# A fifth buffer of attention weights, sums copied before the next rounding, loads moved inside chunks, and a memset moved to VectorE, in a fused attention and mixture-of-experts kernel

## The chip, the cores and the metric

The kernel runs on one core of a Trainium2 chip. The metric is the device time of one execution in microseconds (us). TensorE (PE in the profile, PEld for its weight loads), VectorE (DVE), ScalarE (ACT), GpSimd (POOL) and SyncE (SP) run side by side and wait for each other by semaphores. SP only issues transfers here (DMA); POOL issues those that go by index.

## The reference

```python
B, S, D, d_qk = 8, 2496, 256, 64            # u, v: (B, S, D); z: (B, S, d_qk)
scores = (1.0 / S) * (z @ z.transpose(0, 2, 1))
attn = np.maximum(scores, 0.0) ** 2
x = (u * (attn @ v)).reshape(B * S, D)
out = x.copy()
...                                          # only tokens with x @ w_skip > 0:
e_idx = argmax(xc @ w_gate)                  # one of 8 experts for each token
gate_w = softmax(xc @ w_gate)[e_idx]
out = xc + gate_w * (np.maximum(xc @ w1[e], 0.0) @ w2[e])   # w1: 256x1024, w2: 1024x256
```

All of it is float32. The kernel keeps this precision by splitting each operand of a product into a high part (a cast to the rounded type fp32r) and a low part (the operand less its high part), and by adding three products: high by high, high by low, low by high.

## The kernel before, in words

**Attention.** A batch has 2496 tokens. Its queries are cut into five chunks, four of 512 and one of 448 (`chunks`, 40 in all, called chunk 0 to 4 of batch 0 to 7 below). Its keys are cut into ten pairs of 256 (`NP` = 10), and one chunk with one pair is a step: 400 steps. Steps are numbered from 0 in a chunk, and through the program from 0 to 399; step 80 is step 0 of chunk 3 of batch 1. `ORDER` says in which order a chunk takes its pairs.

The weights of a step, `relu(z z^T / S)^2`, are symmetric. So eight blocks of a batch (`PAIRS`) are computed once, turned by DVE (`keep`, tile `rt`), written to DRAM (`kept`) by SP, and read back (`recall`) when the mirrored block is due. The other steps are computed: `scores` on PE into PSUM (`ps`), relu and square on ACT into `r` (lines 290 and 291). For either kind the rounding follows: `high` casts `r` to `ah` (line 313, on ACT or DVE as `on_act` says) and `low` subtracts on DVE to get `al` (line 317). `attend` (line 341) multiplies `ah` and `al` with `vh` and `vl` into the sums `acc`. Its index d picks one half of the features, so a step calls it twice, and each half has two accumulators (t = 0 and 1), for the two halves of TensorE's rows.

`weights` for a step is called two steps ahead (`LA` = 2), `recall` five steps ahead. At a chunk's end `finish` evacuates: for each d, `part(d, 1)` copies one accumulator to `xrow` by ACT (line 369) and `part(d, 0)` adds the other by DVE (line 371). Only then may the next chunk's `attend` of that d start, because all accumulators of PSUM are in use. Then `mul` multiplies by `ut` (u, loaded one chunk ahead), `rows0` and `rows1` turn the result, and `store` writes it.

**Queues.** Each engine runs its own instructions in the order in which the program was written (`manual_schedule`); `todo` and `at` set work to a half-step number, which is run at the end of that step. So whatever waits holds up all that was written behind it on that engine. This goes for SP too, which issues a transfer only when its target buffer is free.

**Loads.** z and v of the next batch are loaded and split in the background (`load_z`, `load_v`): SP starts the transfer, and seven half-steps later ACT casts (lines 108 and 119) and DVE subtracts (lines 109 and 120). `load_w` does the same for the weights of the experts.

**Routing and experts.** After every second chunk the tokens are routed: `gates` multiplies by the gate's weights on PE, `logits` turns the result to `lg` (lines 431 and 435; where a chunk has 448 tokens, line 434 fills the rest with zeros), `route` finds the expert (`mx` to `hot`), `counts` and `place` find its place in the expert's list (`pre`, and a product with a triangle on PE, line 476), and `put_in` writes token numbers to the lists by POOL. After the attention comes the experts' part, in units of 256 tokens: `h_part` 0 to 3 (line 598), then `y_part` (line 617), with other work put between these parts by `fills`, whose number says after which part. The first unit's tokens were listed early, and the last chunk's routing is done in the fills of this unit.

The loop over steps, as far as it is touched:

```python
if k < NP - 1:                      # all steps but the last of a chunk
    high, low = stage(s + LA)
    high()
    low()
    for d in range(2 if k < NP - 2 else 1):
        attend(b, n, p, d, acc[d], *aa[s], k == 0, False)
```

Of the kernel before, what the change touches and what calls it, by code (L numbers as in the profile page):

```python
# [8 lines left out]
F32 = mybir.dt.float32  # L9
# [8 lines left out]
P = 128  # L18
QC = 512
# [28 lines left out]
def attn_moe(ctx, tc, zT, uT, v, wg, w1, w2, cst, pad, out):  # L48
# [113 lines left out]

    def load_u(ci):
        b, q0, n = chunks[ci]
        uts[ci] = xp.tile([P, 2, QC], F32, name="ut", tag="ut", bufs=4)
        nc.sync.dma_start(uts[ci][:, :, :n], uT[b, :, :, q0 : q0 + n])

    warm = cpool.tile([P, 1], F32, name="warm")
# [83 lines left out]
        return ps  # L252

    def r_tile():
        return ap.tile([P, 2, QC], F32, name="r", tag="r", bufs=4)

    turned_r, puts, step = {}, [], [0]

# [135 lines left out]
    def routing(cis, rows64=True):  # L394
# [27 lines left out]
        def logits():  # L422

            ps = psg.pop()
            lgf = lg.rearrange("p t c -> p (t c)")
            same = all(n % P == 0 for n in ns)
            for g, n in [(0, ns[0])] if same else enumerate(ns):
                full = 32 * (n // P)
                w = P * len(ns) if same else P
                o = g * P  # L430
                nc.vector.transpose(lgf[:full, o : o + w], ps[:full, o : o + w])
                if n % P:
                    k = o + n % P
                    nc.gpsimd.memset(lgf[full : full + 32, k : o + P], 0.0)
                    nc.vector.transpose(lgf[full : full + 32, o:k], ps[full : full + 32, o:k])

        def route():
# [231 lines left out]
    def at(s, f):  # L669

        todo.setdefault(s // 2, []).append(f)
# [3 lines left out]
    def stage(s):  # L675
        if s < len(steps):
            aa[s], high, low = weights(*steps[s], old.pop(s, None))
            return high, low
        return lambda: None, lambda: None
# [16 lines left out]
    def later(s, k, load, *args):  # L696
        def start():
            f = load(*args)
            at(s + k, f)
        at(s, start)  # L700

    for ci, (b, q0, n) in enumerate(chunks):
        s0 = ci * NB
        if ci + 1 < NC:
            at(s0 + 12, lambda ci=ci: load_u(ci + 1))
        if ci == 0:
            first = [(4 * j - 8, j % 2, 3, load_z, j) for j in range(2, NZ)]
            first += [(2 * g - 4, 1, 4, load_v, g) for g in range(2, NB // 2)]
            for s1, _, k, load, j in sorted(first, key=lambda x: x[:2]):
                eng = nc.vector  # L710
                if s1 - k < 0:
                    at(s1, load(0, j, eng))
                else:
                    later(s1 - k, k, load, 0, j, eng)
            at(14, lay_pads)
        if q0 == 0 and b + 1 < B:

            end = s0 + NB * -(-S // QC)
            for j in range(NZ):
                s1 = (s0 + 24, s0 + 44, end - 18, end - 14, end - 10)[j]  # L720
                later(s1, 7, load_z, b + 1, j, nc.vector)
            for g in range(NB // 2):
                s1 = s0 + 21 + 8 * g if g < 7 else (end - 17, end - 14, end - 12)[g - 7]
                later(s1, 7, load_v, b + 1, g, nc.vector)

    s_end = NC * NB
    s_w = s_end - 3 * NB

    def start_w():
        for k, f in enumerate(load_w(0, nc.vector)):  # L730
            at(s_w + 8 + 5 * k, f)

    at(s_w, start_w)

# [20 lines left out]
    for s, (ci, p) in enumerate(steps):  # L755
        b, q0, n = chunks[ci]
        k = s % NP
        step[0] = s
        ahead(s + LA + 3)
        if k == 0:  # L760
            accs[ci] = [[ps_acc.tile([P, QC], F32, name="acc", tag="acc") for _ in range(2)] for _ in range(2)]
        acc = accs[ci]
        if k < NP - 1:
            high, low = stage(s + LA)
            high()
            low()
            for d in range(2 if k < NP - 2 else 1):
                attend(b, n, p, d, acc[d], *aa[s], k == 0, False)
            if k < NP - 2:
                aa.pop(s)  # L770
        else:


            part, mul, rows0, rows1, store = finish(ci)
            attend(b, n, p, 0, acc[0], *aa[s], False, True)
            part(0, 1, acc[0])
            part(0, 0, acc[0])
            high, low = stage(s + LA)
            attend(b, n, steps[s - 1][1], 1, acc[1], *aa.pop(s - 1), False, False)
            if s + LA in known:  # L780

                high()
                low()
                high = low = lambda: None
            attend(b, n, p, 1, acc[1], *aa.pop(s), False, True)
            part(1, 1, acc[1])
            high()
            part(1, 0, acc[1])
            low()
            mul()  # L790
            accs.pop(ci)

            new.append(ci)
            if ci < NC - 1:
                after = [(rows0, 2), (rows1, 3), (store, 4), (store, 5)]
                if ci % 2 == 0:
                    gates, logits, route, counts, gate, place, put_in = routing(new)
                    after = [(gates, 2), (logits, 2), (rows0, 2), (rows1, 3), (route, 4), (counts, 4),
                             (store, 4), (gate, 5), (store, 5), (place, 6)]
                    for t in range(0, 4 * len(new), 2):  # L800
                        f = lambda put_in=put_in, t=t: put_in(t, t + 2)
                        if s + 6 + t < len(steps):
                            after.append((f, 6 + t))
                        else:
                            left.append(f)
                    new = []
                for f, k in after:
                    todo.setdefault(s + k, []).append(f)
            else:
                gates, logits, route, counts, gate, place, put_in = routing(new, False)  # L810
        for f in todo.pop(s, []):
            f()
        put_some()
# [57 lines left out]
    for e in range(E):  # L871
# [3 lines left out]
        for i in range(NFIX):  # L875
# [11 lines left out]
            elif i == 0:  # L887
                add(fills, (0, lambda: turn_pe(pair(0, 1), turned(0, 1))))
                add(fills, (0, gates), (0, rows0), (0, rows1), (0, store), (0, store), (1, logits), (1, route),
                    (2, counts), (2, gate), (3, end_routes), (5, end_lists))  # L890
                add(fills, *zip((0, 2), left))
            elif i == 1:
                add(fills, (1, end_counts), (3, lambda: turn_pe(pair(0, 2), turned(0, 2))), (4, rows(0, 3)), (6, rows(0, 4)))
                add(fills, *zip((1, 3, 5), wq[:3]))
            else:
                add(fills, (1, rows(1, 0)), (3, rows(0, 5)), (4, lambda: turn_pe(pair(0, 3), turned(0, 3))),
                    (5, rows(1, 1)), (6, lambda: load_ids(idts[2], 2, 2 * NSTAT)))
                add(fills, *zip((1, 2, 3, 5, 6), wq[3:]))
# [99 lines left out]
```

## Time and profile before

| what | value |
|---|---|
| time, median of 3 runs | 1835.14 us (1831.97 to 1837.5) |
| profiled execution, time | 1834.64 us |
| its span, first to last instruction | 1832.8 us |
| granted TensorE clock, mean | 0.996 |
| PE busy | 1787.2 us, 98% of the span |
| DVE, ACT, POOL busy | 1182.8, 1159.5, 440.8 us |
| attention, to the last chunk's end | about 0 to 1323 us |
| experts | the rest |

The span is what the profile shows; some 2 us of the execution lie around it. A row of the timeline has the start and the length in us, then the engine, the line of the kernel, the operation, what it writes and reads, and in brackets the idle time of the engine before it and what ended that. A row of waits has the waiting engine with its tile and line, what it waited for, the sum in us, how often, and the longest. Numbers of buffers are left out of names.

### The profile page before, as it was taken

How to read it: one execution, taken by the hardware profiler on the slowest of the kernel's cores; microseconds unless marked ns; L12 is line 12 of the kernel's file. 1: busy time of each engine (PE TensorE's matmuls, PEld its weight loads, DVE VectorE, ACT ScalarE, POOL GpSimd, SP SyncE). 2: the span in 40 equal slices, each digit the busy share in tenths (PEclk: the TensorE clock that was granted, in tenths of full speed). 3: DMA queues.
4: the chain of work that ended last, by engine and by line, in shares of the span. 5: the costliest groups of instructions: out<-in, count | busy, mean ns of one | idle time of the engine just before them, and what ended most of it. 6: DMA issues, size and time to landing. Idle time of an engine off the chain costs nothing. (4 is left out here: it accounts for less than half of the span.)

```text
span 1832.8 us, 40463 instructions
## 1 busy us (share of the span) xinstructions
PE 1787.2 (98%) x15844; PEld 1575.9 (86%) x15844; DVE 1182.8 (65%) x2105; ACT 1159.5 (63%) x1499; POOL 440.8 (24%) x429
## 2 busy tenths in 40 slices
PE   8999999999999999999999999999989999999997
PEld 7888878877887798788879878877889999999997
DVE  6777776876777687678678777867643343334432
ACT  8877876877777687678777876877523233333321
POOL 0102201210220120121012022112254556635621
PEclk9999999999999999999999999999989999999999
DMA  5575687487657847784784787578542233313210
GB/s 185 128 179 138 168 207 190 122 207 187 170 136 196 207 116 193 202 198 119 186 215 108 183 208 187 133 182 197 147 103 76 80 96 106 89 53 94 84 37 26
DMA packets 403766, 267.46 MB, mean 146 GB/s; under 512 B 205859, under 2 KB 334117, under 8 KB 403440
## 3 DMA queue, kind: packets, MB, share of 16 engines
q1 hardware_dynamic: 389440, 240.47, 51.9%
q0 software_dynamic: 13712, 22.99, 4.4%
q8 instruction: 141, 2.31, 0.5%
q14 instruction: 185, 1.52, 0.3%
q10 hardware_dynamic: 288, 0.17, 0.0%
HBM read 145.80 MB, written 118.39 MB: 144 GB/s over the span
## 5 line engine op out<-in xcount | busy, mean ns | idle before, releaser
L341 PE MATMUL acc<-ah,vh 64*128 64x512 f32 (+1 forms) x3120 | 729.5, 387 | 17.5 <-DVE xrow L371 11.4
L341 PE MATMUL acc<-ah,vl 64*128 64x512 f32 (+1 forms) x3120 | 712.7, 385 | 0.0
L317 DVE TENSOR_TENSOR al<-r,ah 128x1024 fp32r<-128x1024 f32 (+3 forms) x464 | 480.0, 1048 | 251.1 <-ACT ah L313 238.8
L341 PE MATMUL acc<-al,vh 64*128 64x512 f32 (+1 forms) x3120 | 562.0, 385 | 3.6 <-DVE al L317 3.2
L341 PEld LDWEIGHTS acc<-ah,vh 64*128 64x128 f32 x3120 | 423.8, 185 | 87.4 <-DVE xrow L371 25.8
L341 PEld LDWEIGHTS acc<-ah,vl 64*128 64x128 f32 x3120 | 424.0, 185 | 45.9 <-DVE vl L120 0.2
L500 POOL DMA_INDIRECT lst<-pair,dest x160 | 192.4, 1203 | 1093.4 <-DVE dest L498 996.1
L290 ACT ACTIVATE r<-ps 128x1024 f32<-128x1024 f32 (+1 forms) x278 | 280.3, 1008 | 225.2 <-PE ps L251 185.3
L341 PEld LDWEIGHTS acc<-al,vh 64*128 64x128 f32 x3120 | 361.3, 185 | 58.6 <-DVE al L317 11.9
L313 ACT CAST ah<-r 128x1024 fp32r<-128x1024 f32 (+3 forms) x381 | 329.1, 891 | 37.8 <-DMA r<-kept 13.2
L291 ACT ACTIVATE r<-r 128x1024 f32<-128x1024 f32 (+1 forms) x278 | 289.9, 1043 | 8.8
L603 ACT ACTIVATE hh<-psh 128x512 fp32r<-128x512 f32 (+1 forms) x172 | 98.7, 584 | 293.2 <-PE psh L598 256.7
L617 PE MATMUL y<-w2t,hh 128*128 128x256 f32 x1328 | 246.5, 287 | 0.0
L598 PE MATMUL psh<-xt,w1h 128*128 128x256 f32 (+1 forms) x1280 | 231.8, 284 | 2.1 <-issue 1.8
L617 PEld LDWEIGHTS y<-w2t,hh 128*128 128x128 f32 x1328 | 208.7, 193 | 1.3 <-issue 1.3
L598 PEld LDWEIGHTS psh<-xt,w1h 128*128 128x128 f32 x1280 | 196.9, 189 | 3.1 <-issue 3.1
L604 DVE SCALAR_TENSOR_TENSOR hl<-psh,hh 128x512 fp32r<-128x512 f32 (+1 forms) x172 | 113.0, 671 | 131.6 <-ACT hh L603 126.0
L617 PE MATMUL y<-w2t,hl 128*128 128x256 f32 x664 | 189.0, 285 | 1.2 <-DVE hl L604 1.2
L598 PE MATMUL psh<-xt,w1l 128*128 128x256 f32 (+1 forms) x640 | 181.1, 283 | 0.0
L268 DVE STREAM_TRANSPOSE rt<-r 128x512 f32<-128x512 f32 x244 | 158.4, 687 | 1.2 <-DMA kept<-rt 1.1
L251 PE MATMUL ps<-zh 64*128 64x512 f32 (+1 forms) x556 | 137.8, 399 | 4.6 <-ACT zh L108 4.6
L251 PE MATMUL ps<-zl,zh 64*128 64x512 f32 (+1 forms) x556 | 135.8, 391 | 0.0
(170 smaller groups left out, 1661.1 us busy)
## 6 DMA issues: line engine op xcount, KB each, us to landing
kept<-rt SPq DMA_DIRECT2D x244, 256.0 KB, 4.9
r<-kept SPq DMA_DIRECT2D x488, 128.0 KB, 4.0
raw<-in_v SPq DMA_DIRECT2D x80, 256.0 KB, 3.8
ut<-in_uT SPq DMA_DIRECT2D x32, 512.0 KB, 5.1
xr<-xrow SPq DMA_DIRECT2D x128, 128.0 KB, 3.1
out<-xrow SPq DMA_DIRECT2D x128, 128.0 KB, 3.2
raw<-in_w SPq DMA_DIRECT2D x64, 256.0 KB, 3.3
zf<-in_zT SPq DMA_DIRECT2D x40, 256.0 KB, 3.8
```

What stands on the lines that cost most here:

```text
L251: nc.tensor.matmul(to, k[h, o : o + P], queries(q, h, n), start=(m == 0), stop=(m == 2))
L268: nc.vector.transpose(t[:, :, 32 * k : 32 * k + 32], r[:, x, :].rearrange("p (m i) -> p m i", i=32))
L290: nc.scalar.activation(r[:, :, :n], ps[:, :, :n], AF.Relu, scale=isc)
L291: nc.scalar.activation(r[:, :, :n], r[:, :, :n], AF.Square)
L313: (nc.scalar.copy if on_act(ci, p) else nc.vector.tensor_copy)(h_, r_)
L317: nc.vector.tensor_sub(l_, r_, f32(h_))
L341: nc.tensor.matmul(acc[t][:, :n], w[h, x, dd], a[h, x, :n], start=(first and t not in halves[:m]), stop=(last and t not in halves[m + 1 :]),)
L500: put = nc.gpsimd.indirect_dma_start(out=lst, out_offset=bass.IndirectOffsetOnAxis(ap=dest[:, t : t + 1], axis=0), in_=pair[:, t, :], in_o ...
L598: nc.tensor.matmul(ps[:, j * W : (j + 1) * W], wt[:, a, o : o + P], x[:, d, :W], start=(m == 0), stop=(m == 5),)
L603: nc.scalar.activation(hh[:, : G * W], ps[:, : G * W], AF.Relu)
L604: nc.vector.scalar_tensor_tensor(hl[:, : G * W], ps[:, : G * W], 0.0, f32(hh[:, : G * W]), op0=ALU.max, op1=ALU.subtract)
L617: nc.tensor.matmul(ys[t], h[:, tt], w2t[f][:, k, :], start=(f == 0 and m == 0 and t % 2 == 0), stop=(f == NF - 1 and m == 2), skip_group_c ...
```

## The change

1. `r` gets five buffers instead of four, `ut` three instead of four; both have 4 KB per partition.
2. At a chunk's last but one step, the rounding (`high`, `low`) of the next chunk's first step is no longer written where it is staged, unless that step is recalled. It is written in the chunk's last step: ahead of `part(0, ...)` where DVE casts, and behind it where ACT casts. That is the case in chunks 2 and 3 of batches 1 to 7, 14 times.
3. The conversions of z and v of the next batch get a table of chunk and step, with none in steps 8, 9, 0 and 1. Before, v was converted in steps 4 and 8 of chunk 1, 2 and 6 of chunk 2, 0, 4 and 8 of chunk 3, and 5 to 7 of chunk 4. The weights of expert 0 likewise.
4. The zeros of `lg` are written by DVE, not POOL.
5. In the first unit of the experts, `place` with the first list writes comes after `y_part` 0 instead of `h_part` 3, and `end_lists` one place later too.

```diff
-        uts[ci] = xp.tile([P, 2, QC], F32, name="ut", tag="ut", bufs=4)
+        uts[ci] = xp.tile([P, 2, QC], F32, name="ut", tag="ut", bufs=3)
...
-        return ap.tile([P, 2, QC], F32, name="r", tag="r", bufs=4)
+        return ap.tile([P, 2, QC], F32, name="r", tag="r", bufs=5)
...
-                    nc.gpsimd.memset(lgf[full : full + 32, k : o + P], 0.0)
+                    nc.vector.memset(lgf[full : full + 32, k : o + P], 0.0)
...
-            end = s0 + NB * -(-S // QC)
-            for j in range(NZ):
-                s1 = (s0 + 24, s0 + 44, end - 18, end - 14, end - 10)[j]
-                later(s1, 7, load_z, b + 1, j, nc.vector)
-            for g in range(NB // 2):
-                s1 = s0 + 21 + 8 * g if g < 7 else (end - 17, end - 14, end - 12)[g - 7]
-                later(s1, 7, load_v, b + 1, g, nc.vector)
+            jobs = [(load_v, 0, 1, 3), (load_z, 0, 1, 6), (load_v, 1, 2, 3), (load_z, 1, 2, 5), (load_v, 2, 2, 7)]
+            jobs += [(load_v, 3, 3, 3), (load_v, 4, 3, 4), (load_v, 5, 3, 6), (load_v, 6, 3, 7)]
+            jobs += [(load_v, 7, 4, 2), (load_z, 2, 4, 3), (load_v, 8, 4, 4), (load_z, 3, 4, 5)]
+            jobs += [(load_v, 9, 4, 6), (load_z, 4, 4, 7)]
+            for load, j, c, k in jobs:
+                later(s0 + c * NB + 2 * k - 7, 7, load, b + 1, j, nc.vector)
...
-        for k, f in enumerate(load_w(0, nc.vector)):
-            at(s_w + 8 + 5 * k, f)
+        for k, f in zip((4, 6, 12, 14, 16, 22, 24, 26), load_w(0, nc.vector)):
+            at(s_w + 2 * k, f)
...
             high, low = stage(s + LA)
-            high()
-            low()
+            if k < NP - 2 or s + LA in known:
+                high()
+                low()
+                high = low = lambda: None
...
+            rest = high, low
         else:
...
             attend(b, n, p, 0, acc[0], *aa[s], False, True)
+
+            high, low = rest
+            if s + 1 < len(steps) and not on_act(*steps[s + 1]):
+                high()
+                low()
+                high = low = lambda: None
             part(0, 1, acc[0])
             part(0, 0, acc[0])
+            high()
+            low()
             high, low = stage(s + LA)
...
-                    (2, counts), (2, gate), (3, end_routes), (5, end_lists))
+                    (2, counts), (2, gate), (4, end_routes), (6, end_lists))
```

ACT at the end of chunk 2 of batch 1, before: `r_3811` is step 79 (the last of the chunk), `r_3861` step 80, `r_3746` the recalled step 81; `vh` is a piece of v for the next batch.

```order
L119 CAST vh_3572<-raw_3570 128x512
L290 ACTIVATE r_3811<-ps_3804 128x1024
L291 ACTIVATE r_3811<-r_3811 128x1024
L313 CAST ah_3814<-r_3811 128x1024
L290 ACTIVATE r_3861<-ps_3854 128x1024
L291 ACTIVATE r_3861<-r_3861 128x1024
L313 CAST ah_3864<-r_3861 128x1024
L369 COPY xrow_3881<-acc_3442 128x512
L313 CAST ah_3905<-r_3746 128x1024
L369 COPY xrow_3881<-acc_3444 128x512
```

The same place in the changed kernel, where `r_3799` is step 79, `r_3851` step 80 and `r_3740` step 81:

```order
L290 ACTIVATE r_3799<-ps_3792 128x1024
L291 ACTIVATE r_3799<-r_3799 128x1024
L313 CAST ah_3802<-r_3799 128x1024
L119 CAST vh_3607<-raw_3605 128x512
L290 ACTIVATE r_3851<-ps_3844 128x1024
L291 ACTIVATE r_3851<-r_3851 128x1024
L369 COPY xrow_3867<-acc_3436 128x512
L313 CAST ah_3882<-r_3851 128x1024
L313 CAST ah_3895<-r_3740 128x1024
L369 COPY xrow_3867<-acc_3438 128x512
```

The first copy of a sum has moved ahead of the cast of step 80, the second still follows the cast of step 81. Of the buffers, which no row here shows: before, step 80's `r` had the place in memory that step 79's had; now it has that of step 78. Likewise step 3 of chunk 4 had the place of step 2, and now has that of step 1.

DVE at the same place, before:

```order
L317 TENSOR_TENSOR al_3762<-r_3758,ah_3761 128x1024
L268 STREAM_TRANSPOSE rt_3690<-r_3758 128x16x32 x2
L120 TENSOR_TENSOR vl_3573<-raw_3570,vh_3572 128x512
L317 TENSOR_TENSOR al_3815<-r_3811,ah_3814 128x1024
L498 TENSOR_SCALAR dest_3438<-df_3719 128x2
L317 TENSOR_TENSOR al_3865<-r_3861,ah_3864 128x1024
L371 TENSOR_TENSOR xrow_3881<-acc_3441,xrow_3881 128x512
L317 TENSOR_TENSOR al_3906<-r_3746,ah_3905 128x1024
L371 TENSOR_TENSOR xrow_3881<-acc_3443,xrow_3881 128x512
L374 TENSOR_TENSOR ut_3308<-xrow_3881,ut_3308 128x1024
```

And in the changed kernel:

```order
L317 TENSOR_TENSOR al_3756<-r_3752,ah_3755 128x1024
L268 STREAM_TRANSPOSE rt_3684<-r_3752 128x16x32 x2
L317 TENSOR_TENSOR al_3803<-r_3799,ah_3802 128x1024
L498 TENSOR_SCALAR dest_3428<-df_3713 128x2
L120 TENSOR_TENSOR vl_3608<-raw_3605,vh_3607 128x512
L371 TENSOR_TENSOR xrow_3867<-acc_3435,xrow_3867 128x512
L317 TENSOR_TENSOR al_3883<-r_3851,ah_3882 128x1024
L317 TENSOR_TENSOR al_3896<-r_3740,ah_3895 128x1024
L371 TENSOR_TENSOR xrow_3867<-acc_3437,xrow_3867 128x512
L374 TENSOR_TENSOR ut_3302<-xrow_3867,ut_3302 128x1024
```

The first add has moved ahead of the `al` of step 80, and `vl` behind the `al` of step 79; the second add still stands behind the `al` of step 81.

PE in the first unit of the experts, before (`psm` is `place`, `y` the unit's output):

```order
L598 MATMUL psh_18806<-xt0_18289,w1l_17854 128x256
L476 LDWEIGHTS tri_127
L476 MATMUL psm_18821<-hot_18672,tri_127 128x32
L476 LDWEIGHTS ones_129
L476 MATMUL psm_18821<-pre_18673,ones_129 128x32
L617 MATMUL y_18702<-w2t_17984,hh_18703 128x256 x2
```

And in the changed kernel:

```order
L617 MATMUL y_18702<-w2t_18043,hh_18703 128x256 x2
L617 MATMUL y_18702<-w2t_18043,hl_18704 128x256
L476 LDWEIGHTS tri_127
L476 MATMUL psm_18833<-hot_18672,tri_127 128x32
L476 LDWEIGHTS ones_129
L476 MATMUL psm_18833<-pre_18673,ones_129 128x32
L617 MATMUL y_18702<-w2t_18340,hh_18703 128x256 x2
```

The twelve matmuls of `y_part` 0 now stand ahead of the two that read `hot` and `pre`.

## The prediction

> **What bounds the kernel now.** I read the page first, then who waited for whom, then the rows around the longest waits of TensorE.
>
> ```profile
> PE 1787.2 (98%) x15844; PEld 1575.9 (86%) x15844; DVE 1182.8 (65%) x2105; ACT 1159.5 (63%) x1499; POOL 440.8 (24%) x429
> ```
> ```profile
> ACT r L290 <- DVE al L317: 20.5, 10, 2.4
> ...
> PE acc L341 <- DVE xrow L371: 11.4, 15, 1.0
> ...
> PE psm L476 <- DVE hot L451: 6.4, 1, 6.4
> ...
> DVE mx L442 <- POOL lg L434: 5.9, 1, 5.9
> ...
> PE acc L341 <- ACT xrow L369: 3.3, 7, 0.5
> PE acc L341 <- DVE al L317: 3.2, 12, 0.3
> ...
> PE psm L476 <- DVE pre L457: 1.2, 1, 1.2
> ...
> PE psm L409 <- ACT r L290: 1.0, 1, 1.0
> ```
>
> TensorE (PE) is busy 98% of the span, so only its waits can give time back, and the change removes no TensorE work. Its waits are few and lie in four places: at chunks' ends it waits for the sums to be copied out of `acc` (11.4 + 3.3), at the entrance to the experts it waits once for `hot` and `pre` (6.4 + 1.2), and now and then for `al`, or for a `ps` buffer. The wait for `hot` is VectorE's (DVE's) wait for the memset on GpSimd (POOL), 5.9. The 20.5 us that ScalarE (ACT) waits for `al` is a wait for a buffer of `r`.
>
> I count a loss from start to start of matmuls, since the idle column begins only at a modelled end: below, 277.88 follows 276.50 by 1.38, and 0.88 of it is called idle.
>
> **Chunks' ends (2 to 3 and 1 to 2 of batches 1 to 7).** First ACT, then DVE, then PE, chunk 2 to 3 of batch 1:
>
> ```profile
> 269.57 1.05 ACT L313 CAST ah<-r 128x1024 fp32r<-128x1024 f32 x1
> 272.77 1.02 ACT L290 ACTIVATE r<-ps 128x1024 f32<-128x1024 f32 x1 [2.14 <-DVE dest L498]
> ...
> 274.92 1.05 ACT L313 CAST ah<-r 128x1024 fp32r<-128x1024 f32 x1
> 275.87 0.58 ACT L369 COPY xrow<-acc 128x512 f32<-128x512 f32 x1
> 276.35 1.05 ACT L313 CAST ah<-r 128x1024 fp32r<-128x1024 f32 x1
> ```
> ```profile
> 271.46 1.22 DVE L317 TENSOR_TENSOR al<-r,ah 128x1024 fp32r<-128x1024 f32 x1
> ...
> 277.14 0.68 DVE L371 TENSOR_TENSOR xrow<-acc,xrow 128x512 f32<-128x512 f32 x1
> 277.74 1.21 DVE L317 TENSOR_TENSOR al<-r,ah 128x1024 fp32r<-128x1024 f32 x1
> 278.87 0.68 DVE L371 TENSOR_TENSOR xrow<-acc,xrow 128x512 f32<-128x512 f32 x1
> ```
> ```profile
> 272.73 0.73 PE L341 MATMUL acc<-al,vh 64*128 64x512 f32 x4
> ...
> 276.50 0.50 PE L341 MATMUL acc<-ah,vh 64*128 64x512 f32 x1 [0.52 <-ACT xrow L369]
> 277.88 0.50 PE L341 MATMUL acc<-ah,vh 64*128 64x512 f32 x1 [0.88 <-DVE xrow L371]
> ...
> 278.22 0.63 PE L341 MATMUL acc<-ah,vh 64*128 64x512 f32 x2
> 278.46 0.63 PE L341 MATMUL acc<-ah,vl 64*128 64x512 f32 x2
> ...
> 279.61 0.72 PE L341 MATMUL acc<-ah,vl 64*128 64x512 f32 x2
> ```
>
> ACT's relu of step 80 starts at 272.77, right after the `al` of step 79 (271.46 + 1.22 = 272.68): its `r` lies in that step's buffer. So ACT idles 2.14 us (the row names the tiny `dest` that follows), the cast and the copy of the first sum come late, and PE starts the new chunk in pieces at 276.50 and 277.88; its second half runs only from 279.61, after the second add (278.87 + 0.68). Unhindered, two matmuls of 512 columns start every 0.23 to 0.24 us (278.22, 278.46), so an `attend` call (12 matmuls) takes 1.38, and that of the last pair (9) 1.04.
>
> With five buffers step 80 takes the buffer of step 78, and the wait goes. What is late next? I take effective times from these starts: relu and square 2.15 (272.77 to 274.92), cast 0.95, copy 0.48, `al` 1.13, add 0.60. In the new order ACT does relu, square, copy, cast 80, cast 81, second copy; DVE does add, `al` 80, `al` 81, second add. Let S be the end of the square and T the end of the first sum. The second add ends at max(S, T) + 0.48 + 0.95 + 1.05 + 1.13 + 0.68 and about 0.15 of hand-overs, or max(S, T) + 4.45. PE would come to it at T + 3.6 (1.38 + 1.04 left of the old chunk, 1.38 of the new one, less 0.2 because T is an end). So the first sum costs nothing any more, but the second still costs 0.9 to 1.1 per chunk's end: `al` 81 stands ahead of its add, as before. The reordering alone gives the second add nothing (in the old order it ends at S + 4.35); what helps is that S comes earlier and that no `vh`, `vl` stands between.
>
> Batch 1, 2 to 3: the cast of step 79 leaves ACT at 270.52; a conversion of v (now in step 7) takes 0.6, relu and square 2.15: S = 273.2. T was 273.3 (the row at 272.73: its fourth matmul starts 0.2 later and takes 0.4) and becomes 272.9, for PE's wait for `al` there, 0.3 and a restart, goes too: the `vl` that DVE did ahead of that `al` comes behind it. New end 277.7 against 279.6: **1.9**. The other three kinds:
>
> ```profile
> 239.65 0.62 ACT L119 CAST vh<-raw 128x512 fp32r<-128x512 f32 x1
> ...
> 243.25 0.69 DVE L371 TENSOR_TENSOR xrow<-acc,xrow 128x512 f32<-128x512 f32 x1
> ...
> 403.96 1.05 ACT L313 CAST ah<-r 128x1024 fp32r<-128x1024 f32 x1
> ...
> 408.52 0.68 DVE L371 TENSOR_TENSOR xrow<-acc,xrow 128x512 f32<-128x512 f32 x1
> ...
> 433.39 1.06 ACT L313 CAST ah<-r 128x1024 fp32r<-128x1024 f32 x1
> ...
> 441.91 0.68 DVE L371 TENSOR_TENSOR xrow<-acc,xrow 128x512 f32<-128x512 f32 x1
> ```
>
> Batch 1, 1 to 2: S = 239.65 less the cast's 0.95, 238.7, T a little later; end 243.3 against 243.94: **0.65**. Batch 2, 1 to 2: S and T at about 403.95 (the square ends as the row's cast starts); 408.4 against 409.2: **0.75**. Batch 2, 2 to 3: ACT leaves the cast at 434.35, with a v and 2.15 S = 437.1; 441.5 against 442.6: **1.1**. Odd and even batches repeat these (routing falls into other chunks). Batch 7 has no v to bring, so its 1 to 2 gives nothing. Sum: 4 x 1.9 + 3 x 1.1 + 3 x 0.65 + 3 x 0.75 = **15.1**. In batch 0 one such wait goes, **0.4**.
>
> **The last chunk of a batch.**
>
> ```profile
> 317.05 1.09 DVE L317 TENSOR_TENSOR al<-r,ah 128x896 fp32r<-128x896 f32 x1 [3.02 <-ACT ah L313]
> ...
> 334.25 0.48 PE L341 MATMUL acc<-ah,vh 64*128 64x448 f32 x2 [0.32 <-DVE ah L313]
> ...
> 335.44 0.67 PE L341 MATMUL acc<-al,vh 64*128 64x448 f32 x3 [0.30 <-DVE al L317]
> ```
>
> Step 3's `r` again lay in the buffer of the step before, so DVE idled 3.02 and then worked without a pause until PE stood waiting. Here, and in two waits for `al` and `ah` of even batches, the fifth buffer lets DVE begin some 2.5 us earlier, and two conversions (0.6 each) are moved into that idle time: odd batches gain 0.32 + 0.30 and what lies around them by starts, about 1.0, three times; even ones 0.5, four times (part of the 3.2 for `al`); batch 7 the 1.0 for `ps`. Together **6.0**. The ends are 0, if the conversion of v that now comes in step 6 is as much in the way as the one in step 7 was, and 7; I take the sum, since more of DVE's idle time (3.02) is there than the two conversions need (1.2).
>
> **Loads and buffers of u.** Per conversion, ACT pays 0.5 to 0.6 and DVE 0.6; 15 per batch stay 15. Chunk 3 gets one more, chunk 1 one less. The cover is DVE's 35% idle; without it each costs its 0.6. SP issues the loads behind the recalls of `r`:
>
> ```profile
> 302.30 10.77 SPq L280 DMA_DIRECT2D r<-kept  x12
> ```
> ```profile
> ut<-in_uT SPq DMA_DIRECT2D x32, 512.0 KB, 5.1
> ```
>
> They waited there 10.77 us for buffers, which gets shorter; each load keeps a lead of four steps, over 10 us, so I take 0. u is loaded at step 6 and read at step 9, 8 us later, against 5.1 to land; with three buffers the one needed was freed in step 2. Without that cover the multiply would wait for the load, some 5 us. I take 0. The weights of expert 0, now converted in the middle of the last three chunks, cost the same engines as much as before: 0.
>
> **The entrance to the experts.** DVE, POOL, then the windows (time, then busy of PE, PEld, DVE, ACT, POOL, clock, DMA share, GB/s):
>
> ```profile
> 1327.91 0.26 DVE L435 STREAM_TRANSPOSE lg<-psm 32x64 f32<-32x64 f32 x1
> 1334.12 0.19 DVE L442 TENSOR_REDUCE mx<-lg 128x4 f32<-128x32 f32 x1 [5.94 <-POOL lg L434]
> ...
> 1333.88 0.20 POOL L434 MEMSET lg<- 32x64 f32 x1
> ```
> ```profile
> 1336.90:1342.00 5.10, 5.10 (x25) 5.10 (x25) 1.98 (x11) 0.18 (x1) 1.95 (x2) 0.51 0.00 0
> 1342.00:1344.90 2.90, 2.90 (x26) 2.90 (x25) 0.00 (x0) 0.00 (x0) 1.94 (x2) 1.00 0.07 9
> ```
>
> POOL's memset stood behind eight list writes. On DVE it costs between 0.05 (nothing but its place) and 0.26 (the transpose of that size); I take 0.1; the seven others stand in DVE's idle time. The Trainium skill, "VectorE: DVE Perf Modes", section "Zero memsets can be issued as uint32 (trn2)", says one cycle per element, an estimate of 0.07 for 64; the sum would not move. Then `mx` runs at about 1328.3, `hot` 1.3 later, `pre` after one `hl` and its own chain at about 1331.0. PE, which now does the first 12 `y` matmuls first (12 x 2.90/26 = 1.3), comes at 1330.4: a wait of 0.5 where 6.4 + 1.2 stood, **7.1**. With `place` a copy on ACT and eight small operations on DVE move behind those `y`, with `end_lists` two list writes on POOL and two loads on SP behind the last `y`; all still come earlier than now, since what they wait for does, and the first rows fetched by these lists belong to the unit after next: 0. Behind it 25 matmuls ran at a granted clock of 0.51, in 5.10 us against 25 x 0.112 = 2.8: **2.3** more, which I take as gone with the wait. The rule for it is in the Trainium skill, "TensorE: Matmul & The Clock Gate", section "Part 1: The HAM clock gate (the "warmup" mystery)": about 3.4 us of idling halve the clock. The trace agrees that 0.88 us at 277.88 did not, for the next pair came 0.34 later and the one after it 0.24 later; by proportion to the wait 0.15 of the 2.3 would stay, by the rule none.
>
> **The sum.** 15.1 + 0.4 + 6.0 + 7.1 + 2.3 = 30.9. The profiled run took 1834.6, so 1803.7; it lies 0.5 under the median shown (1835.1), so **1804**.
>
> **Rivals.** *The chunks' ends keep their loss*: the second add's wait swallows all. For it speaks that its queue is unchanged; against, S + 4.45 from earlier S. 15.1 less: 1819. *The second sum's wait goes as well*, if recalls land so early that `al` 81 is done before it is needed; 14 x 1.0 more: 1790; against it stands DVE's order. *Slower: conversions are late.* Ten of a batch's 15 now stand in chunks 3 and 4, where their 0.6 on DVE may push `al` past its matmuls; all ten on the path in seven batches is 42, or 1846; it decides from 4.4 us per batch, over seven of the ten. Against it: the 3.02 idle and the 2.14 on ACT. *The entrance keeps a wait of 5*, if `place` or the lists are late: with a clock that falls again, 7 less, 1811.
>
> **How the numbers follow.** Forecast (1797 to 1811) 0.68; ends keep their loss 0.10; both sums free 0.07; entrance 0.07; slower 0.04; several half-way, near 1825 to 1840, 0.04. Range 1796 to 1819. A measurement here tells 0.3%, 5.5 us, from no change. Faster 0.91, same 0.04, slower 0.05.
>
> **What would show it.** Right: no ACT wait for `al` over 1 us at chunks' ends, PE's wait for `xrow` once per such end (14 in all, near 0.9 by starts, at the second sum); `mx` waiting for nothing, granted clock 1.00 at the first `y`; no PE wait for `ah` at the end of chunk 4. Wrong: PE waits for `al` in chunks 3 and 4, for `vh`, `vl` or `ut`, or a new wait for fetched rows behind the lists.

## The result, and the profile after

| | kernel before | changed kernel |
|---|---|---|
| time, median | 1835.03 us (1831.97 to 1837.5, 4 runs) | 1804.41 us (1803.4 to 1807.72, 4 runs) |
| ratio | 1 | 0.9837, 95% interval 0.9818 to 0.9857 |
| span of the profiled execution | 1832.8 us | 1802.5 us |

The forecast was 1804, within 1796 to 1819. The change gained 30.6 us, 30.3 of it in the two profiles. First the page after, engines' busy time, and PE's waits, as the rows of before were read:

```profile
PE 1772.0 (98%) x15844; PEld 1579.0 (88%) x15844; DVE 1183.1 (66%) x2113; ACT 1161.6 (64%) x1499; POOL 439.2 (24%) x421
```
```profile
PE acc L341 <- DVE xrow L371: 10.3, 15, 0.8
...
PE acc L341 <- DVE al L317: 2.7, 12, 0.3
...
PE psm L476 <- DVE pre L457: 0.6, 1, 0.6
```

The waits of PE for `hot` (6.4) and for ACT's `xrow` (3.3) are gone, and ACT's wait of 20.5 for `al` has no row any more. The wait for DVE's `xrow` stays, 15 times as before.

To see where the time went I cut both profiles at the same instructions: ACT's second copy of a sum at the end of the first chunk, of the 39th and of the 40th, and the first `y` of the experts. Kernel before, then the changed one (ACT, then PE):

```profile
45.44 0.58 ACT L369 COPY xrow<-acc 128x512 f32<-128x512 f32 x1 [0.19 <-PE acc L341]
1291.94 0.59 ACT L369 COPY xrow<-acc 128x512 f32<-128x512 f32 x1 [0.84 <-PE acc L341]
1321.74 0.53 ACT L369 COPY xrow<-acc 128x448 f32<-128x448 f32 x1 [1.69 <-PE acc L341]
```
```profile
1336.86 0.56 PE L617 MATMUL y<-w2t,hh 128*128 128x256 f32 x1
```
```profile
44.13 0.59 ACT L369 COPY xrow<-acc 128x512 f32<-128x512 f32 x1 [0.17 <-PE acc L341]
1272.71 0.59 ACT L369 COPY xrow<-acc 128x512 f32<-128x512 f32 x1 [0.84 <-PE acc L341]
1301.36 0.53 ACT L369 COPY xrow<-acc 128x448 f32<-128x448 f32 x1 [1.74 <-PE acc L341]
```
```profile
1308.51 0.28 PE L617 MATMUL y<-w2t,hh 128*128 128x256 f32 x1
```

| stretch | before | after | gain | forecast |
|---|---|---|---|---|
| to the first chunk's second copy | 45.44 | 44.13 | 1.31 | 0 |
| from there to the 40th chunk's | 1276.30 | 1257.23 | 19.07 | 21.5 |
| from there to the first `y` | 15.12 | 7.15 | 7.97 | 7.1 |
| first `y` to the end of the span | 495.9 | 494.0 | 1.9 | 2.3 |

The first row isn't the change's doing: this stretch took 43.83 us in another profile of the kernel before, and 45.67 in another of the changed kernel. PE's last wait for `pre` (0.61, below) stands behind the first `y` now, and so in the last row; counted with the entrance, the last two gains are 7.4 and 2.5.

A chunk's end in the changed kernel, chunk 2 to 3 of batch 1 (the place of the prediction's rows), ACT, DVE and PE:

```profile
270.23 1.06 ACT L291 ACTIVATE r<-r 128x1024 f32<-128x1024 f32 x1
271.19 0.57 ACT L369 COPY xrow<-acc 128x512 f32<-128x512 f32 x1
271.66 2.00 ACT L313 CAST ah<-r 128x1024 fp32r<-128x1024 f32 x2
```
```profile
271.79 0.69 DVE L371 TENSOR_TENSOR xrow<-acc,xrow 128x512 f32<-128x512 f32 x1 [0.94 <-ACT xrow L369]
272.74 2.36 DVE L317 TENSOR_TENSOR al<-r,ah 128x1024 fp32r<-128x1024 f32 x2 [0.25 <-ACT ah L313]
275.02 0.68 DVE L371 TENSOR_TENSOR xrow<-acc,xrow 128x512 f32<-128x512 f32 x1
```
```profile
274.60 0.39 PE L341 MATMUL acc<-ah,vh 64*128 64x512 f32 x1
275.76 0.50 PE L341 MATMUL acc<-ah,vh 64*128 64x512 f32 x1 [0.76 <-DVE xrow L371]
```

The square is done at 271.19 (S), and the second add ends at 275.02 + 0.68 = 275.70, S + 4.51 where the forecast had 4.45. PE comes at 274.60 and goes on at 275.76; less the 0.23 of an unhindered step that is a loss of 0.93, where 0.9 to 1.1 was forecast.

The entrance to the experts, DVE, then PE, then a window of time, in which PE's granted clock is the third figure from the end:

```profile
1307.58 0.11 DVE L434 MEMSET lg<- 32x64 f32 x1
1307.70 0.26 DVE L435 STREAM_TRANSPOSE lg<-psm 32x64 f32<-32x64 f32 x1
1307.99 0.19 DVE L442 TENSOR_REDUCE mx<-lg 128x4 f32<-128x32 f32 x1
```
```profile
1309.93 0.19 PE L476 MATMUL psm<-hot,tri 128*128 128x32 bf16 x1
1310.73 0.18 PE L476 MATMUL psm<-pre,ones 128*128 128x32 bf16 x1 [0.61 <-DVE pre L457]
```
```profile
1311.00:1316.00 5.00, 5.00 (x44) 5.00 (x44) 2.61 (x12) 0.12 (x1) 0.97 (x1) 1.00 0.26 54
```

The memset takes 0.11 (forecast 0.1), `mx` waits for nothing, PE waits 0.61 (forecast 0.5), and the clock stays at 1.00.

### The profile page after: what moved, and what is told of

The parts are those of the page before. It is cut to its first block, busy times and chain, and to the rows that moved or that the text cites. A ratio compares the mean times of both kernels' runs of the same rounds, so it can differ in the third digit from the quotient of the medians.

```text
span 1802.5 us, 40479 instructions
## 1 busy us (share of the span) xinstructions
PE 1772.0 (98%) x15844; PEld 1579.0 (88%) x15844; DVE 1183.1 (66%) x2113; ACT 1161.6 (64%) x1499; POOL 439.2 (24%) x421
```

## The experiments

They ran in four groups, each on a chip of its own beside runs of the kernel before. That kernel took 1840.1, 1841.9, 1833.7 and 1839.9 us (medians), so ratios count, and times only inside a group. This table cuts all profiles as above: attention from the first to the 39th second copy, then to the first `y`, then to the end of the span.

| kernel | group | time | ratio to before (95%) | attention | to `y` | experts |
|---|---|---|---|---|---|---|
| before | first | 1835.0 | 1 | 1246.50 | 44.92 | 495.9 |
| before (e8) | 2 | 1842.4 (one run) | 1 | 1248.87 | 47.86 | 499.9 |
| changed | first | 1804.4 | 0.9837 (0.9818 to 0.9857) | 1228.58 | 35.80 | 494.0 |
| changed (e5) | 2 | 1817.9 | 0.9868 (0.9851 to 0.9885) | 1228.60 | 40.57 | 502.6 |
| e1 fifth buffer | 1 | 1819.7 | 0.9889 (0.9873 to 0.9906) | 1228.10 | 45.62 | 499.6 |
| e2 conversions' steps | 1 | 1835.1 | 0.9979 (0.9966 to 0.9993) | 1245.24 | 47.10 | 496.4 |
| e3 order | 1 | 1836.6 | 0.9983 (0.9974 to 0.9993) | 1244.31 | 46.17 | 499.1 |
| e4 memset | 1 | 1839.8 | 1.0000 (0.9990 to 1.0009) | 1249.56 | 46.98 | 497.0 |
| e12 memset again | 4 | 1839.7 | 0.9998 (0.9986 to 1.0009) | 1246.42 | 47.70 | 500.3 |
| e6 changed, POOL memset | 2 | 1819.5 | 0.9876 (0.9859 to 0.9892) | 1230.00 | 42.39 | 502.3 |
| e7 changed, `low` late | 2 | 1807.7 | 0.9811 (0.9794 to 0.9827) | 1218.58 | 40.57 | 504.3 |
| e9 changed, old order | 3 | 1806.0 | 0.9848 (0.9831 to 0.9864) | 1227.75 | 35.79 | 495.9 |
| e10 changed, old steps | 3 | 1807.6 | 0.9858 (0.9842 to 0.9875) | 1230.18 | 35.79 | 493.2 |
| e11 e7, lists late | 3 | 1805.9 | 0.9854 (0.9838 to 0.9871) | 1218.18 | 35.79 | 505.3 |

### e1: the fifth buffer alone

```diff
-        uts[ci] = xp.tile([P, 2, QC], F32, name="ut", tag="ut", bufs=4)
+        uts[ci] = xp.tile([P, 2, QC], F32, name="ut", tag="ut", bufs=3)
...
-        return ap.tile([P, 2, QC], F32, name="r", tag="r", bufs=4)
+        return ap.tile([P, 2, QC], F32, name="r", tag="r", bufs=5)
```

> The kernel before with five buffers of r and three of ut, nothing else. My theory: the wait of ScalarE for al (20.5 us) goes by itself, so the first sum of a chunk's end is no longer waited for, and the second add ends earlier by the same amount as in the full change; some conversions of v still stand at the ends of chunk 1 and cost what the reordering does not. Of the 30.9 of the sum I expect the 2 to 3 ends (4 x 1.9 + 3 x 1.1 = 10.9), half of the 1 to 2 ends (2 of 4.2), and two thirds of the last chunks (4 of 6): 17, so about 1818 (1814 to 1822). Rival: without the reordering the copy of the sum stands behind the casts, so PE waits as before: no more than 8, 1827 or above. The wait for hot (6.4) stays in both.

It gained 20.4 us where 17 was expected, and the rival fell. In its profile the attention is in sum as short as in the whole change (marks of ACT, then ACT's wait for `al`, 20.5 before):

```profile
45.51 0.59 ACT L369 COPY xrow<-acc 128x512 f32<-128x512 f32 x1 [0.17 <-PE acc L341]
1273.61 0.59 ACT L369 COPY xrow<-acc 128x512 f32<-128x512 f32 x1 [0.84 <-PE acc L341]
```
```profile
ACT r L290 <- DVE al L317: 3.1, 2, 1.9
```

1273.61 less 45.51 is 1228.10, against 1228.58 with everything. So the buffer alone brings, in sum, what the order, the steps and the buffer bring together. Batch by batch the two differ. From the last chunk's second copy of one batch to that of the next, e1 takes 162.19, 162.71 and 162.67 for batches 1, 3 and 5, the changed kernel 161.75, 162.25 and 162.33; for batches 2, 4 and 6 e1 takes 159.92, 159.91 and 159.95, the changed kernel 160.37, 160.37 and 160.39. The other edits gain some 0.4 in an odd batch and lose as much in an even one.

### e2 and e3: the steps of the conversions alone, the order alone

e2 is the kernel before with these lines of the change:

```diff
-            for g in range(NB // 2):
-                s1 = s0 + 21 + 8 * g if g < 7 else (end - 17, end - 14, end - 12)[g - 7]
...
+            for load, j, c, k in jobs:
+                later(s0 + c * NB + 2 * k - 7, 7, load, b + 1, j, nc.vector)
...
-            at(s_w + 8 + 5 * k, f)
+            at(s_w + 2 * k, f)
```

> The kernel before with the new steps of the conversions of z, v and the expert's first weights, nothing else. My theory: with four buffers the 20.5 us of ScalarE stay nearly whole, so the chunk's ends give only the casts of vh and vl that no longer stand there: 2 to 3 us at the ends of chunk 1, 1 to 2 at the end of chunk 2, 1 to 2 in the last chunk, less about 1 for conversions that come late in chunk 3: 5, so about 1830 (1827 to 1833). Rival: the conversions were the whole reason of the waits at the ends: 15 or more, 1820 or below.

e3 is the kernel before with these, shown in part:

```diff
+            if k < NP - 2 or s + LA in known:
+                high()
+                low()
+                high = low = lambda: None
...
             part(0, 1, acc[0])
             part(0, 0, acc[0])
+            high()
+            low()
```

> The kernel before with the sums copied ahead of the next rounding, nothing else. My theory: the reordering gives the second add nothing (it ends 4.45 after the later of square and first sum, 4.35 in the old order), so although the first sum is copied earlier and PE's first wait at an end goes, PE waits as much longer for the second: at most 3 us faster, 1832 to 1836. Rival: the copies' place in the queues is what makes PE wait, and most of the 15.1 of the chunks' ends comes from it: 1820 to 1823.

e2 is 5.0 us faster, as expected, though not everywhere as expected: the last chunks of odd batches, booked with a gain, grew from 30.3 to 30.9. e3 is 3.6 faster, a little more than the 3 expected at most. ACT's wait for a buffer of `r` stays nearly whole in either; the rows are ACT's sum in e2, and step 80's relu in e3, batch 1:

```profile
ACT r L290 <- DVE al L317: 18.8, 10, 2.4
```
```profile
272.65 1.03 ACT L290 ACTIVATE r<-ps 128x1024 f32<-128x1024 f32 x1 [2.13 <-DVE dest L498]
```

### e4: the memset alone

```diff
-                    nc.gpsimd.memset(lgf[full : full + 32, k : o + P], 0.0)
+                    nc.vector.memset(lgf[full : full + 32, k : o + P], 0.0)
```

> The kernel before with the zeros of the logits written by VectorE, nothing else (the place of the lists stays). My theory: the waits for hot and pre (6.4 + 1.2) become one of about 2.0, because the turn of gates into places starts 0.1 after the logits, and the 2.3 us that PE ran at a granted clock of 0.51 go: 5.6 + 2.3 = 7.9, so about 1827 (1825 to 1829). Rival: another part of the chain, or POOL's list writes behind it, is late next, and the loss of clock stays in proportion to a wait of over 4: 4 us or less, 1831 or above.

Neither: nothing was gained at all. The profile shows a wait that the first profile of the kernel before does not have (ACT, then the last of POOL's eight list writes):

```profile
1337.03 0.60 ACT L603 ACTIVATE hh<-psh 128x512 fp32r<-128x512 f32 x1 [8.02 <-issue]
```
```profile
1335.35 0.97 POOL L500 DMA_INDIRECT lst<-pair,dest  x1 [0.30 <-issue]
```

`hh` needs only PE's `psh` matmuls, and all twelve of them are recorded as started from 1328.40 to 1329.75. DVE's `hl` and the logits come behind `hh`, so the memset, early or late, was hidden.

### e5 and e8: the changed kernel and the kernel before, unchanged, for their profiles on one chip

> The changed kernel as it is, on the chip of this group. The memset alone gave nothing (1839.75 against 1840.11): in its profile ScalarE stands 8.02 us before the hh of the entrance at 1337.03, although PE's psh matmuls that it reads began at 1328.40, and it goes on when GpSimd's eight list writes end (1336.32). In the changed kernel's first profile the same hh stood at 1305.99 amid the list writes and waited 1.99. Theory A: that stall belongs to the chip or the run, not to the kernel. Then here the changed kernel either has it too (about 1810, DVE free of the memset but hh late), or this chip is without it (1804). Theory B: the full change removes the stall by the other places of its work: 1804 where the kernel before is at 1840.

> The kernel before, unchanged, for its profile on this chip beside the others. Theory A: if ScalarE's stall of the entrance belongs to the chip, it stands here too (some 8 us before the same hh, ended with the list writes), hidden behind VectorE's wait for the memset, or in its place; then the wait for hot stays near 6.4 and the memset can gain nothing. Theory B: hh waits 1.57 as in the first profile and only the memset's wait is there; then the stall is caused by the edit.

The kernel before has the same stall on this chip, and there `mx` waits for no memset (ACT, then DVE, in e8):

```profile
1335.89 1.09 ACT L603 ACTIVATE hh<-psh 128x512 fp32r<-128x512 f32 x2 [8.18 <-remote]
```
```profile
1337.81 0.18 DVE L442 TENSOR_REDUCE mx<-lg 128x4 f32<-128x32 f32 x1
```

The changed kernel has it as well, in two parts (e5): first at the copy of the last sum, whose last matmuls are recorded at 1302.51, then at its first `hh`:

```profile
1306.37 0.53 ACT L369 COPY xrow<-acc 128x448 f32<-128x448 f32 x1 [4.59 <-PE pst L569]
1310.03 0.60 ACT L603 ACTIVATE hh<-psh 128x512 fp32r<-128x512 f32 x1 [3.12 <-remote]
```

So theory A of both holds: the stall goes with the chip, not with the edit. All profiles of groups 1, 2 and 4 have it, none of the first pair and of group 3. The changed kernel takes 4.8 us more before the first `y` on this chip, 3.45 of it up to that copy (32.10 for the last chunk against 28.65), 8.6 more in the experts, and no more up to the 39th copy (1228.60 against 1228.58). That the stall causes the 8.6 too is not shown: there PE waits 8.1 us against 3.5, 3.9 of it for nothing that the profile shows, and its granted clock is 0.93 over the first 50 us (1.00 in the first profile). The gain on this chip is 24.0 instead of 30.6.

### e6: the changed kernel with the memset on POOL

```diff
-                    nc.vector.memset(lgf[full : full + 32, k : o + P], 0.0)
+                    nc.gpsimd.memset(lgf[full : full + 32, k : o + P], 0.0)
```

> The changed kernel with the zeros of the logits written by GpSimd again, all else kept. Theory A (the memset's wait is worth what the prediction said): GpSimd's last list write ends at 1312.2 of the first profile, so hot comes at 1313.6 instead of 1309.3 and pre at 1315.0 instead of 1310.6; 4.3, and up to 2.3 of clock: 4 to 7 slower than the changed kernel. Theory B (the entrance waits for ScalarE's hh until the list writes end, whoever writes the zeros): within 1 of the changed kernel on this chip.

1.6 slower than e5, with intervals that overlap; 1.8 more before the first `y`. Nearer to theory B: the first `hh` waits 6.69 here. But behind it the memset still holds up `mx`, by 1.65: POOL writes the zeros at 1316.01, and `mx` starts at 1316.23.

### e7: `low` of the recalled step after the second add

```diff
             if s + LA in known:
 
                 high()
-                low()
-                high = low = lambda: None
+                high = lambda: None
```

`low` is then issued by the call that already stands behind `part(1, 0, ...)`.

> The changed kernel with one more move: in a chunk's last step VectorE's al of a recalled step comes after the add of the second sum, not ahead of it; ScalarE's cast ah stays ahead. My theory: the second add ends at max(S, T) + 3.3 instead of + 4.45, PE comes to it at T + 3.6, so its 14 waits of 0.9 to 1.1 go and al still is in time (its matmuls come a step later): 14 x 0.9 = 12.6 less than the changed kernel, about 1791 where that is at 1804. Rival: the al, 1.2 later, is now itself late for its matmuls, and PE waits for al instead: no gain, or a loss of up to 4.

10.2 us faster than e5, 12.6 expected. PE's waits for `xrow` fall from 10.4 us to 0.4; below that sum, then DVE and PE at the end of chunk 2 of batch 1:

```profile
PE acc L341 <- DVE xrow L371: 0.4, 1, 0.4
```
```profile
271.70 1.23 DVE L317 TENSOR_TENSOR al<-r,ah 128x1024 fp32r<-128x1024 f32 x1 [0.26 <-ACT ah L313]
273.13 0.69 DVE L371 TENSOR_TENSOR xrow<-acc,xrow 128x512 f32<-128x512 f32 x1 [0.21 <-ACT xrow L369]
273.74 1.21 DVE L317 TENSOR_TENSOR al<-r,ah 128x1024 fp32r<-128x1024 f32 x1
```
```profile
273.57 0.81 PE L341 MATMUL acc<-ah,vh 64*128 64x512 f32 x2
273.89 0.72 PE L341 MATMUL acc<-ah,vl 64*128 64x512 f32 x2
```

The add now stands between the two `al`, ends at 273.82, and PE goes through without a wait. Waits for `al` did not grow (2.7 us against 2.6). All of the gain is attention: 10.0. This kernel beats both others.

### e9 and e10: the changed kernel without the order, and without the steps

e9 takes the lines of e3 out of the changed kernel, e10 those of e2 (both shown in part):

```diff
...
-            high, low = rest
-            if s + 1 < len(steps) and not on_act(*steps[s + 1]):
...
             part(0, 1, acc[0])
             part(0, 0, acc[0])
-            high()
-            low()
```

> The changed kernel with the sums copied in the old order (casts and al ahead of them), all else kept. The fifth buffer by itself brought the last chunk of attention as early as the whole change did (last attend at 1301.85, of which the start-up 45.51, against 1302.52 with 45.67), so I now think that the new order and the new steps of the conversions are worth nothing in sum once the buffer is there. Theory A: the new order gives the second add nothing: within 2 us of the changed kernel (1817.9 on such a chip: 1816 to 1820). Theory B: the order is worth 5 or more and the new steps of the conversions cost as much: 1823 or above.

```diff
...
-            for load, j, c, k in jobs:
-                later(s0 + c * NB + 2 * k - 7, 7, load, b + 1, j, nc.vector)
...
+            for g in range(NB // 2):
+                s1 = s0 + 21 + 8 * g if g < 7 else (end - 17, end - 14, end - 12)[g - 7]
```

> The changed kernel with the old steps of the conversions of z, v and the first weights, all else kept. Theory A: with five buffers the idle time of VectorE and ScalarE at the ends covers the conversions wherever they stand; what chunk 2 loses (a vh, vl ahead of the second add: 0.3 to 0.5 in a batch), chunk 3 wins back (its waits for al, 0.2 to 0.4): within 2 us of the changed kernel. Theory B (the prediction's): vh and vl at the ends cost 4 to 7 in sum: 1822 to 1825.

The changed kernel did not run in this group. Of the ratios, 0.9848 lies within its interval of the first runs (0.9818 to 0.9857), 0.9858 just outside, so the times favour theory A for e9 and don't settle e10. The attention of the profiles is nearer to theory A in both. With five buffers the attention takes 1228.10 (neither, e1), 1227.75 (new steps alone, e9), 1230.18 (new order alone, e10) and 1228.58 (both). So with the buffer the steps give 0.4 to 1.6, and the order costs 0.8 to 2.1. Single profiles of one attention differ by up to 3 (the kernel before, above), so the sums alone would not settle this; but the place repeats. End of chunk 1 of batch 2, the changed kernel, ACT and PE:

```profile
397.49 1.06 ACT L291 ACTIVATE r<-r 128x1024 f32<-128x1024 f32 x1
399.22 0.59 ACT L369 COPY xrow<-acc 128x512 f32<-128x512 f32 x1 [0.67 <-DMA r<-kept]
399.70 2.00 ACT L313 CAST ah<-r 128x1024 fp32r<-128x1024 f32 x2
```
```profile
402.91 0.39 PE L341 MATMUL acc<-ah,vh 64*128 64x512 f32 x1
403.80 0.50 PE L341 MATMUL acc<-ah,vh 64*128 64x512 f32 x1 [0.51 <-DVE xrow L371]
```

The same in e9:

```profile
399.60 1.05 ACT L313 CAST ah<-r 128x1024 fp32r<-128x1024 f32 x1
400.56 0.58 ACT L369 COPY xrow<-acc 128x512 f32<-128x512 f32 x1
```
```profile
403.94 0.94 PE L341 MATMUL acc<-ah,vh 64*128 64x512 f32 x2
404.39 0.72 PE L341 MATMUL acc<-ah,vl 64*128 64x512 f32 x2
```

In the new order ACT stands 0.67 until PE has finished the first sum, copies it, and only then casts (the row names a transfer, but the copy needs the sum, whose last matmuls start at 398.68). In the old order the cast fills that time. PE loses 0.89 less 0.23 in the one and 0.45 less 0.23 in the other. From this chunk's second copy to the next one's it is 31.98, 32.00 and 32.01 in batches 2, 4 and 6 of the changed kernel, and 31.53, 31.54 and 31.53 in e9. In odd batches the new order gains there: 34.13 in batches 3 and 5, and 34.24 in e9.

### e11: e7 with six of eight list writes behind the first `y`

```diff
-                        if s + 6 + t < len(steps):
+                        if s + 6 + t < len(steps) - 3:
...
-                add(fills, *zip((0, 2), left))
+                add(fills, *zip((4, 4, 5, 5), left))
```

> The kernel of the low after the second add, and in it six of the eight list writes that GpSimd has at the entrance are issued behind the first y matmuls (with the writes of the last tokens), not ahead. In the profiles of these chips ScalarE's hh of the entrance starts up to 8 us after TensorE's psh matmuls, in five of six runs within 2 us of the end of a row of list writes. Theory A: TensorE's signals are held back while list writes follow each other; moved away, hh starts at once, the first y comes 7.5 after the last attend and not 12.3: 4 to 5 faster than 1807.7, 1803, if the hold does not come back behind y. Theory B: the hold comes back with the writes, later: y and psh of the first unit wait, 1806 to 1809. Theory C: list writes have nothing to do with it: hh as late as before, 1807.7 within 2.

None of the three was tested, as this chip has no stall: `hh` is on time in e9 and e10 of the group too. Instead it shows the price of late lists (DVE, then PE):

```profile
1324.47 0.17 DVE L549 COPY go<-idt 128x2 int32<-128x2 int32 x1 [11.05 <-DMA idt<-lst]
```
```profile
1326.75 0.51 PE L617 MATMUL y<-w2t,hl 128*128 128x256 f32 x1 [4.02 <-DVE hl L604]
```

DVE stood 11.05 for a list read back, with `hl` behind it, and the experts took 505.3 against 493.2 and 495.9 in its group. That ate about the 10.4 by which its attention is shorter than the changed kernel's.

### e12: the memset alone, again

The edit is e4's.

> The kernel before with the zeros of the logits written by VectorE, once more, since chips differ: on two of them (kernel before at 1840 and 1842) ScalarE's hh of the entrance waited up to 8 us for TensorE's signal and the memset hid behind it; on two others (1835 and 1834) it did not. Theory A: on a chip of the second kind (before at about 1834 to 1835) the waits for hot and pre (6.4 + 1.2) become one of about 2.0 and the 2.3 of clock go: 7.9, about 1827. Theory B: even there hh or GpSimd's list writes hold the entrance and nothing is gained: within 2 of before. On a chip of the first kind (before at 1840 or above) both give no change, as at first.

It fell on a chip with the stall (the kernel before at 1839.9), and gave nothing again. PE's wait for `hot`, then ACT:

```profile
PE psm L476 <- DVE hot L451: 1.6, 1, 1.6
```
```profile
1333.25 1.08 ACT L603 ACTIVATE hh<-psh 128x512 fp32r<-128x512 f32 x2 [7.62 <-remote]
```

The wait for `hot` did shrink from 6.4 to 1.6, about the 2.0 expected, but the first `y` came no earlier (47.70 after the mark, 47.86 in e8): `hh` and `psh` ahead of it were late.

## Why the prediction was right, and where its steps were not

**The total** held by two errors that cancel: attention gave 2.4 less than forecast, while the start-up (1.3, chance), the entrance and the clock together gave 1.8 more. That it was met within 0.4 us is luck; on the chip of e5 the same change gave 24.0. Of attention, the last chunks gave 7.5 where 6.0 was forecast, and the three chunks ahead of them 11.7 where the ends and batch 0 were to give 15.5. In batch 0 these three took 0.2 longer, where 0.4 was to go.

**The fifth buffer** was the right cause at the chunks' ends: e1 alone brings ACT's wait from 20.5 to 3.1 and gives all of the some 18 us of the 39 chunks, while e2 and e3 alone leave it.

**The reordering** is where a step failed: "The reordering alone gives the second add nothing (in the old order it ends at S + 4.35)". The two formulas were compared as if S, the end of the square, were the later one. With five buffers S comes early and T, the first sum, is the later at some ends; the new order then pays T in full, while the old one casts in that time. So the new order takes about 0.4 at such an end (e9), gives 0.1 at the same end of odd batches, and brings no gain in sum. By these profiles that part of the change could have been left out.

**The conversions** got credit that they did not have in sum. The terms 0.65 and 0.75 at the ends of chunk 1, and part of the 6.0 of the last chunks, were booked on `vh` and `vl` leaving; e1, which moves none, reaches the same attention, and its last chunks are as short (29.13 in odd batches, 27.58 in even ones, as in the changed kernel). Batch 1 gained 3.24 (164.99 to 161.75 between its bounding second copies) where 3.55 was forecast, batch 2 2.25 against 2.35. The rival of late conversions shows at its foot only: a new wait for `al` of 0.17 at 454.79, in chunk 3 of an even batch, whose interval grew from 32.70 to 32.96; e10, with the old steps, has 32.52 there.

**The second sum's wait** stayed, once at each of the 14 ends: 0.66 to 0.69 at three ends of even batches, 0.89 to 0.94 at the others, 12.1 in all. The rival that it goes was not the change's, but e7 shows its cause (`al` of the recalled step, ahead of the add) and its worth: 10.0 rather than 14. That it is less fits the 12.1, and what e7 leaves of them, 0.1 or 0.2 at each end, 2.1 in all.

**The entrance** came out by its terms (7.4 and 2.5 against 7.1 and 2.3). No run isolates it on a chip without the stall. What speaks for it is the first pair of profiles, where the 5.94 of `mx` and the 0.51 of the clock are gone, and that e9 and e10, which lack the order or the steps, keep the 35.79 before `y`; that leaves the memset, the place and the buffer, and of the 9.12, 1.15 is the last chunk's (29.80 to 28.65), which in other batches the buffer gives alone (29.13 at batch 1 in e1 as in the whole change). On chips with the stall the memset alone gave nothing, twice, and within the change it was worth some 1.6 by the times of e5 and e6, whose intervals overlap. So the part of the gain at the entrance is argued from the rows, not shown by a run.

**Costs taken as nothing**, the loads behind recalls and `ut` with three buffers, showed no wait of PE for `vh`, `vl` or a load of u.

## What to carry to other kernels

Give the starved tile its buffer first and look again: here one buffer did what three edits were meant to do, and the other two gave in odd batches what they took in even ones. When work is moved ahead of a wait, compare the two orders once with each input as the late one, since the removal of the old delay decides which it is. Then look what still stands in the queue ahead of the instruction that PE waits for: moving one subtraction behind one add was worth 10 us more.

## What the runs showed of the hardware

The same kernel took 1804.4 us on one chip and 1817.9 on another, the kernel before 1833.7 to 1841.9. In three of the five groups ScalarE stood 3 to 8 us before an `hh` of the entrance, although TensorE's matmuls for it are recorded as started long before, and in most of these profiles TensorE itself shows waits for nothing (`issue`) among them. It is TensorE's signal that comes late, not ScalarE: in e8 three groups of `psh` start at 1326.37, 1327.86 and 1329.22, and the trace has the semaphore updates that tell of them at 1335.87, 1336.00 and 1336.12. In the first profile of the changed kernel such updates come within 0.02 us of the modelled end of a group. Whether the matmuls or only their signals were late, the trace does not show. In e2, e3, e4, e8 and e12, which have eight list writes in a row there, it went on 0 to 1.9 us after the last of them ended (e3 1331.10 after 1331.08, e12 1333.25 after 1331.40). That TensorE's signals are held back while list writes follow each other fits this. Against it, the late copy of e5 went on at 1306.37, in the middle of a list write (1305.69 to 1306.66). It wasn't shown: the run meant for it fell on a chip without the stall, and why chips differ stays open.

On a chip with the stall the clock fell after shorter waits, too: in e1 the granted clock was 0.50 from 1308 to 1314 and from 1320 to 1324.5, behind waits of PE of 2.32 us (1306.54) and of 2.14 and 1.20 (1317.82, 1319.20). Waits of up to 0.95 us at its chunks' ends did not lower it (1.00 from 230 to 1250). As recorded starts ran ahead of the signals there, the true waits may have been longer.

The VectorE memset of 32x64 took 0.11 us. The estimate of 0.07 that the prediction drew from the Trainium skill, "VectorE: DVE Perf Modes", section "Zero memsets can be issued as uint32 (trn2)", which counts one cycle per element, is lower; the measurement decides.
